# An attention-and-MLP kernel: own-engine waits in front of GpSimd's longer operations

## The chip, the cores and the metric

The kernel runs on one core of a Trainium2 chip. Its time is the device time of one execution, in microseconds. The engines are named as in the profile: PE is TensorE (matmuls; PEld its weight loads), DVE is VectorE, ACT is ScalarE, POOL is GpSimd, and SP is SyncE, which here issues most DMAs.

## What is computed

An "hourglass" attention over 8 batches, 8 heads, 576 positions of 64 channels, whose output is the input of an MLP over 4608 tokens:

```python
q_d = q.reshape(B, H, Sd, 4, D).mean(axis=3)      # k_d, v_d alike: 144 positions
out_up = np.repeat(sm_attn(q_d, k_d, v_d), 4, axis=2)
mask = np.abs(pos[:, None] - pos[None, :]) < 4    # a band of 7 positions
scores = np.where(mask, scale * q @ k.T, -1e9)
attn = softmax(scores)
x = transpose(out_up + attn @ v)                  # 4608 x 512
h = x @ w_in                                      # w_in 512 x 2048
out = (h * sigmoid(h)) @ w_out                    # w_out 2048 x 512
```

## The kernel before

**Tiling.** Two heads of a batch make a pair (32 pairs), two pairs a quad (16 quads). For a pair, q, k and v are loaded by SP into float32 staging buffers (`qs`, `ks`, `vs`; three, three and two of them) and cast to bf16 (`qb`, `kb`, `vb`) by POOL, ScalarE or VectorE. TensorE transposes q and k (from quad 9 on a DMA does), VectorE sums groups of four positions (`qd`, `kd`), TensorE makes the band's scores and the coarse scores in PSUM (tiles `duo`), and ScalarE exponentiates them into `Pt` and `Pd`. VectorE multiplies `Pt` by the band mask in place (`do_mask`, L606 to 611): both its inputs, `Pt` and `mask_bf`, lie in SBUF, 128 x 1152 bf16, 32 times in all. TensorE sums the columns; VectorE takes the reciprocal, which is spread over the partitions by matmuls for the first four quads and, after that, by a store to DRAM (`scr`) and a load back (`Rb`), both issued by SP. TensorE then forms P times V, VectorE multiplies it by `Rb` into `xo`, and POOL adds the two attentions and writes the transposed activations `xT` (`do_add`, L761 to 773).

From quad 4 on the coarse v comes from a second load of v (`vq`) and three additions and a memset on POOL (`castv`, L456 to 465): one addition of 112 x 768 into `vq`, two into `vd`, a memset of part of `vd`.

**The MLP** takes 512 tokens at a time, nine times: 16 blocks `g1` of four matmuls (tile `hps`, at the start also `ops`), a tanh on ScalarE (`th`) and a product on VectorE (`gT`, L794), then 16 blocks `g2` into `ops`, a copy into `osb`, and the store of the output. Its matmuls fill TensorE between those of the attention.

**The order** is not written by hand. Tasks are recorded into one stream per engine by a planner (`choose`, L970 to 985) that estimates each task's start from costs in the code and takes the earliest, with offsets from a table (`TUNE`). The planner treats POOL's operations and the mask product as excluding each other (`self.lock`), in its estimates only.

**Waits** are worked out when an operation is recorded (`Prog.op`, L134 to 200). It collects `deps`, pairs of an earlier operation and a flag; `_dep` (L120 to 132) turns them into semaphore waits. A dependence on the same engine becomes a wait only where the flag is set:

```python
        if d.eng == op.eng and not d.dsem and not forced:
            return
        if know.get(dom, -1) >= val:
            return
```

The flag is set for a tile that the operation reads and an earlier one of its own engine wrote: so the second step of `castv` already waits for the first on POOL's own semaphore. Its third step, which reads the same data as the second, does not wait, and neither does a cast behind a cast. The planner's start estimate `t` (L156 to 159) takes only dependences on other engines and on DMAs into account.

Each operation has a planned `cost` in ns: a POOL cast 680 (L449) or 740 (L454), the steps of `castv` 1900, 1030 and 400 (L460 to 465), an `xT` addition 200 + 1.8 for each column (L772). POOL also issues the loads of the MLP's weights (`load_w`, L823 to 834).

Of the kernel before, what the change touches and what calls it, by code (L numbers as in the profile page):

```python
# [52 lines left out]
class Prog:  # L53
# [38 lines left out]
    def _dma(self, op, eng, t, cost, tau):  # L92

        if t > self.ring_t:
            self._drain(self.rings, self.ring_t, t)
            self.ring_t = t
        full = sum(x[1] / x[2] for x in self.rings[eng]) > 116
        self.rings[eng].append([op, cost, tau, t + (700 if eng == "POOL" else 0)])
        rings = {e: [list(x) for x in q] for e, q in self.rings.items()}
        now, free = self.ring_t, None  # L100
        while any(rings.values()):
            if free is None and (not full or sum(x[1] / x[2] for x in rings[eng]) <= 80 + cost / tau):
                free = now
            now = self._drain(rings, now, now + 400)
        return free or now
# [14 lines left out]
    def _dep(self, op, d, know, forced):  # L120
        if d is op:
            return
        dom, val = (d.dsem, d.dval) if d.dsem else (d.eng, d.pos)
# [4 lines that stand above are left out]
        d.inc = True  # L128
        op.waits = [w for w in op.waits if not (w[0] == dom)] + [(dom, val, d)]
        for k, v in d.K.items():  # L130
            if know.get(k, -1) < v:
                know[k] = v

    def op(self, eng, fn, r=(), w=(), dma=None, cost=0, issue=450, tau=90, lock=False):  # L134
        op = Op(eng, fn)
        op.cost = cost
        op.pos = len(self.streams[eng])
        know = self.know[eng]
        deps = []
        for x in r:  # L140
            if x.psum:
                deps += [(o, False) for e, o in x.last.items() if e != eng]
            else:
                deps += [(o, True) for o in x.writers]
        for x in w:
            if x.psum:
                deps += [(o, False) for e, o in x.last.items() if e != eng]
            else:
                rd = x.readers + ([op] if x in r else [])
                if rd:  # L150
                    x.prev, x.readers, x.writers = rd + x.writers, [], []
                deps += [(o, dma is not None or eng != "PE") for o in x.prev]
                if dma is not None:
                    deps += [(o, True) for o in x.writers if o.dsem != dma]
        deps = [(d, f) for d, f in deps if d is not op]
        t = self.free[eng]  # L156
        for d, f in deps:
            if d.eng != eng or d.dsem:
                t = max(t, d.end + self.LATENCY[d.eng])
        if dma:  # L160
            op.t0 = t
            t += issue if eng == "SP" else 650 if eng == "ACT" else 800
            self.free[eng] = max(t, self._dma(op, eng, t, cost, tau) if eng != "POOL" else t)
            if eng == "POOL":
                self._dma(op, eng, t, cost, tau)
        else:
            if lock or eng == "POOL":
                t = max(t, self.lock)
            op.t0 = t
            self.free[eng] = op.end = t + cost * (1.3 if eng == "PE" and t < 40000 else 1)  # L170
        if lock or (eng == "POOL" and not dma):
            self.lock = op.end
        op.deps = [d for d, f in deps]
        op.tag = self.tag
        deps.sort(key=lambda df: -(df[0].pos if not df[0].dsem else 1 << 30))
        for d, f in deps:
            self._dep(op, d, know, f)
        op.waits = [
            w for w in op.waits
            if not any(v is not w and v[2].K.get(w[0], -1) >= w[1] for v in op.waits)  # L180
        ]
        for x in r:
            if x.psum:
                x.last[eng] = op
            elif x not in w:
                x.readers.append(op)
        for x in w:
            if x.psum:
                x.last[eng] = op
            else:  # L190
                x.writers.append(op)
        op.K = dict(know)
        if dma:
            self.dcount[dma] = self.dcount.get(dma, 0) + 16
            op.dsem, op.dval = dma, self.dcount[dma]
            op.K[dma] = op.dval
        else:
            op.K[eng] = op.pos
        self.streams[eng].append(op)
        return op  # L200
# [848 lines left out]
```

## Time and profile before

| what | us |
|---|---|
| median of 4 runs (lowest, highest) | 374.1 (373.28, 375.96) |
| the profiled execution's own time | 373.87 |
| its span, from the first to the last instruction | 372.1 |
| PE busy, of the span | 340.2 |
| DVE, ACT, POOL busy | 233.3, 217.7, 156.0 |
| POOL's idle time before xT additions, waiting for `xo` of DVE | 59.5 |
| the 32 mask products on DVE, L608 | 29.5 |

The busy shares tell how full each engine is over the whole span. In a list of groups or a timeline, each line gives a start or a count, a duration, the engine, the line of the code, the operation, the tiles as output<-input with their shapes, and in brackets the idle time of that engine just before, with what ended it. Several like instructions in a row are merged and marked x2, x3 and so on. The view of waits gives, for each pair of a waiting group and what it waited for, the total in us, how often, and the longest. The page also has a row of the granted TensorE clock over 40 slices of 9.3 us each:

```profile
PEclk9989699999999999999999999999999999999999
DMA  8999989779999999999996899795144010001012
```

The digits are tenths of full speed and, below, tenths of the 16 DMA engines' time: DMA is near full for the first 200 us.

### The profile page before, as it was taken

The page shows a single profiled execution, that of the slowest core. Times are in us where ns is not written, and L with a number is a line of the kernel's source. Part 1 is how long each engine was busy: PE and PEld are TensorE (multiplying, and loading weights), DVE is VectorE, ACT ScalarE, POOL GpSimd, SP SyncE. Part 2 cuts the span into 40 slices and gives each one's busy share as a digit, 9 for nine tenths or more (in the row PEclk, how much of TensorE's full clock was granted, in tenths as well). Part 3 has the DMA queues.
Part 4 walks back from the last instruction along what each step waited for, and adds up shares of the span by engine and source line. Part 5 has one row for each costly group of instructions (what it writes and reads, how often), then busy time and mean ns, then how long its engine had stood idle before and what let it go on. Part 6 is the DMA issues. An engine that isn't in the chain of part 4 may idle for free.

```text
span 372.1 us, 8309 instructions
## 1 busy us (share of the span) xinstructions
PE 340.2 (91%) x3456; PEld 211.4 (57%) x3498; DVE 233.3 (63%) x375; ACT 217.7 (59%) x362; POOL 156.0 (42%) x203
## 2 busy tenths in 40 slices
PE   0756898999989999999999999999999999999996
PEld 0645566666645665566556565556566555555542
DVE  4688489868668956795598469967765333333310
ACT  4886685576628853886588647766743343443321
POOL 7926672786278429643782285066113000000000
PEclk9989699999999999999999999999999999999999
DMA  8999989779999999999996899795144010001012
GB/s 240 319 361 340 180 224 260 154 202 265 202 242 248 255 256 256 247 234 260 266 235 176 186 196 167 191 168 125 34 116 105 30 56 28 30 28 56 30 56 85
DMA packets 85093, 66.13 MB, mean 178 GB/s; under 512 B 62784, under 2 KB 64832, under 8 KB 85056
## 3 DMA queue, kind: packets, MB, share of 16 engines
q1 hardware_dynamic: 80832, 59.31, 66.5%
q0 software_dynamic: 4224, 6.29, 7.4%
q8 instruction: 27, 0.44, 0.5%
q14 instruction: 10, 0.08, 0.1%
HBM read 53.67 MB, written 9.88 MB: 171 GB/s over the span
## 4 chain that ended last, share of the span: by engine, by line
PE 74%; DMA 9%; DVE 6%; POOL 4%; SPq 3%; issue 2%; ACT 2%; DVEq 0%; POOLq 0%; ACTq 0%
PE ops L538 32%; PE hps L538 31%; PE duo L538 10%; DMA Rb<-scr 4%; DMA scr<-rr 2%; DVE Pt L608 2%; PE duo L548 2%; DMA vq<-in_v_dram 2%; DMA qs<-in_q_dram 1%; SPq L411 1%; POOL xT L771 1%; POOL vq L460 1%; DVE xo L751 1%; POOL vd L462 1%; ACT Pt L585 0%
## 5 line engine op out<-in xcount | busy, mean ns | idle before, releaser
L538 PE MATMUL hps<-xT,w_in_sb 128*128 128x512 f32 x544 | 171.1, 437 | 3.7 <-DVE gT L794 2.4
L794 DVE SCALAR_TENSOR_TENSOR gT<-th,hps 128x512 bf16<-128x512 f32 x136 | 92.5, 682 | 80.9 <-ACT th L792 80.4
L538 PE MATMUL ops<-w_out_bf,gT 128*128 128x512 bf16 x534 | 137.7, 381 | 3.4 <-issue 1.3
L792 ACT ACTIVATE th<-hps 128x512 f32<-128x512 f32 x136 | 81.6, 600 | 97.2 <-PE hps L538 95.1
L538 PEld LDWEIGHTS hps<-xT,w_in_sb 128*128 128x128 f32 x544 | 99.7, 190 | 32.4 <-DVE gT L794 3.3
L538 PEld LDWEIGHTS ops<-w_out_bf,gT 128*128 128x128 bf16 x576 | 46.6, 98 | 68.9 <-issue 28.8
L771 POOL TENSOR_TENSOR xT<-xo 128x576 fp32r<-128x576 f32 (+2 forms) x40 | 39.7, 1004 | 59.6 <-DVE xo L754 59.5
L608 DVE TENSOR_TENSOR Pt<-Pt,mask_bf 128x1152 bf16<-128x1152 bf16 x32 | 29.5, 925 | 6.1 <-ACT Pt L600 5.5
L375 ACT ACTIVATE osb<-ops 128x512 f32<-128x512 f32 x30 | 18.0, 599 | 22.1 <-PE ops L538 22.0
L585 ACT ACTIVATE Pt<-duo 128x912 bf16<-128x912 f32 x29 | 26.9, 929 | 5.7 <-PE duo L538 5.6
L751 DVE TENSOR_TENSOR xo<-duo,Rb 128x456 f32<-128x456 f32 x30 | 18.8, 628 | 14.4 <-DMA Rb<-scr 12.8
L572 DVE TENSOR_REDUCE qd<-qT 128x144 bf16<-128x576 bf16 x29 | 21.4, 746 | 8.4 <-ACT qT L375 5.2
L379 POOL CAST qb<-qs 128x576 bf16<-128x576 f32 x24 | 18.0, 762 | 17.4 <-DMA qr<-qb 15.2
L460 POOL TENSOR_TENSOR vq<-vq 112x768 f32<-112x768 f32 x12 | 22.0, 1836 | 5.3 <-DMA vq<-in_v_dram 5.3
L462 POOL TENSOR_TENSOR vd<-vq 112x384 bf16<-112x384 f32 (+1 forms) x24 | 23.6, 1004 | 1.3
L572 DVE TENSOR_REDUCE kd<-kT 128x144 bf16<-128x576 bf16 x29 | 21.2, 743 | 0.9 <-ACT kT L375 0.7
L379 POOL CAST kb<-ks 128x576 bf16<-128x576 f32 x26 | 16.8, 666 | 11.4 <-PE duo L548 6.2
L379 POOL CAST vb<-vs 128x640 bf16<-128x640 f32 x10 | 7.2, 721 | 24.7 <-PE duo L538 23.6
L375 ACT ACTIVATE vb<-vs 128x640 bf16<-128x640 f32 x20 | 14.5, 736 | 3.3 <-PE duo L538 1.8
L538 PEld LDWEIGHTS duo<-qT,kT 64*128 64x128 bf16 x286 | 8.3, 97 | 12.0 <-issue 4.7
L375 ACT ACTIVATE kT<-kr 128x576 bf16<-128x576 bf16 x12 | 14.9, 1239 | 0.0
L548 PE MATMUL duo<-id_bf,qb 128*128 128x128 bf16 x72 | 5.9, 232 | 9.7 <-ACT qb L375 9.0
(123 smaller groups left out, 332.7 us busy)
## 6 DMA issues: line engine op xcount, KB each, us to landing
vs<-in_v_dram SPq DMA_DIRECT2D x60, 160.0 KB, 5.4
out_dram<-osb SPq DMA_DIRECT2D x36, 256.0 KB, 2.7
Rb<-scr SPq DMA_DIRECT2D x24, 360.0 KB, 5.7
qs<-in_q_dram SPq DMA_DIRECT2D x29, 288.0 KB, 5.2
ks<-in_k_dram SPq DMA_DIRECT2D x29, 288.0 KB, 5.3
vq<-in_v_dram SPq DMA_DIRECT2D x24, 288.0 KB, 5.1
w_in_sb<-in_moe_w_in_dram POOLq DMA_DIRECT2D x4, 1024.0 KB, 12.7
w_out_bf<-in_moe_w_out_dram POOLq DMA_DIRECT2D x4, 512.0 KB, 7.5
```

The costliest lines, as they stand in the source:

```text
L375: fn = lambda e: e.activation(dst, src, AF.Copy, scale=1.0 if scale is None else scale)
L379: fn = lambda e: e.tensor_copy(dst, src)
L460: pool(lambda g: g.tensor_tensor(t, t, z[0:112], ALU.add), r=[R("vq"), R("vqz")], w=[R("vq")], cost=1900)
L462: pool(lambda g, a=a, n=n: g.tensor_tensor(vd[m][0:n, a, :, :, :].rearrange("p i h d -> p h i d"), x[0:n], y[0:n], ALU.add), r=[R("vq"), R ...
L538: return P.op("PE", lambda t: t.matmul(out_, lhsT, rhs, start=start, stop=stop, skip_group_check=True), r, w, cost=cost)
L572: P.op("DVE", lambda e: e.tensor_reduce(dst[j][:, 0:144], src[y][:, :].rearrange("p (g r) -> p g r", r=4), mybir.AxisListType.X, ALU.add), ...
L585: later("ACT", f"e1{p}", [(lambda e: e.activation(Pt[m][:, :, 0:456], D[:, :, 0:456], AF.Exp, scale=0.125), bk, [R(f"P{m}")], 930)], bk)
L608: P.op("DVE", lambda e: e.tensor_tensor(Pt[m][:, :, :], Pt[m][:, :, :], mask_bf[:, :].unsqueeze(1).to_broadcast([128, 2, S_]), ALU.mult), ...
L751: later("DVE", f"pa{p}", [(lambda e: e.tensor_tensor(xo[x][:, 0:456], D[:, 0, 0:456], Rb[u][:, 0:456], ALU.mult), [bk[0], R(f"Rb{u}")], [R ...
L771: P.op("POOL", lambda e, dst=dst, in0=in0, in1=in1: e.tensor_tensor(dst, in0, in1, ALU.add), r=[R(f"xo{x}")], w=xblk(kc, t, e_), cost=200 ...
L792: later("ACT", f"th{n}", [(lambda e: e.activation(th[tb][:, :], hp, AF.Tanh, scale=0.5), [hr], [R(f"th{tb}")], 597)], [hr], pre=[f"st{n - ...
L794: later("DVE", f"st{n}", [(lambda e: e.scalar_tensor_tensor(gT[j % 2][:, f, :], th[tb][:, :], 1.0, hp, ALU.add, ALU.mult), [hr, R(f"th{tb} ...
```

## The change

A POOL operation with a planned cost of 400 or more gets a forced dependence on the operation recorded in front of it on POOL, unless that one is a DMA issue. It then waits, besides all that it waited for, until POOL's semaphore tells that the operation in front has finished.

```diff
@@ -152,6 +152,9 @@
                 deps += [(o, dma is not None or eng != "PE") for o in x.prev]
                 if dma is not None:
                     deps += [(o, True) for o in x.writers if o.dsem != dma]
+        if eng == "POOL" and cost >= 400 and not dma and self.streams["POOL"] and not self.streams["POOL"][-1].dsem:
+
+            deps.append((self.streams["POOL"][-1], True))
         deps = [(d, f) for d, f in deps if d is not op]
         t = self.free[eng]
         for d, f in deps:
```

Since the planner's estimate leaves out dependences on the same engine, the recorded streams keep their order on every engine, and only POOL's operations have other waits than before: of the 191 that are not DMA issues, 129 have one more. Lines behind the change have numbers larger by three.

## The prediction

> **What bounds the kernel now.** I read the busy shares first, then TensorE's (PE's) waits, then the timeline where one of them ends.
>
> ```profile
> PE 340.2 (91%) x3456; PEld 211.4 (57%) x3498; DVE 233.3 (63%) x375; ACT 217.7 (59%) x362; POOL 156.0 (42%) x203
> ```
>
> PE is busy for 340.2 of 372.1 us; POOL, which the change touches, for 42%. From 141 us on PE has no wait above 0.16 us (its busy time is 19.6 to 19.9 in each 20 us). So POOL moves the end only through PE's waits before 141 us, or by making a new one. The view of PE's waits (us in total, times, longest):
>
> ```profile
> PE duo L538 <- DVE Pt L608: 3.5, 2, 2.1
> ...
> PE hps L538 <- DVE gT L794: 2.4, 2, 1.3
> ...
> PE hps L538 <- DVE Pt L608: 1.7, 1, 1.7
> ...
> PE hps L538 <- POOL xT L771: 0.7, 1, 0.7
> ```
>
> 5.2 us are waits for the mask product on VectorE (DVE), L608. The tile's view gives its durations, least, median and longest:
>
> ```profile
> L608 DVE TENSOR_TENSOR Pt<-Pt,mask_bf x32: 742/750/3340, 17.6 to 270.6; 128x1152 bf16<-128x1152 bf16 x32
> ```
>
> Section 5 has 29.5 us for the 32; at 0.75 they would take 24.0. The excess is 5.5 us, and one product holds 2.59 of it. The timeline there:
>
> ```profile
> 53.54 0.73 POOL L379 CAST vb<-vs 128x640 bf16<-128x640 f32 x1
> ...
> 53.97 3.34 DVE L608 TENSOR_TENSOR Pt<-Pt,mask_bf 128x1152 bf16<-128x1152 bf16 x1 [0.79 <-ACT Pt L600]
> 54.20 0.68 POOL L379 CAST qb<-qs 128x576 bf16<-128x576 f32 x1
> ...
> 54.81 0.67 POOL L379 CAST kb<-ks 128x576 bf16<-128x576 f32 x1
> ...
> 55.42 0.66 POOL L379 CAST qb<-qs 128x576 bf16<-128x576 f32 x1
> ...
> 56.03 0.66 POOL L379 CAST kb<-ks 128x576 bf16<-128x576 f32 x1
> ...
> 56.64 1.19 POOL L379 CAST qb<-qs 128x576 bf16<-128x576 f32 x1
> ...
> 57.83 0.74 DVE L608 TENSOR_TENSOR Pt<-Pt,mask_bf 128x1152 bf16<-128x1152 bf16 x1
> ...
> 58.63 0.44 PE L538 MATMUL duo<-Pt,onesZ 128*32 128x72 bf16 x32 [1.45 <-DVE Pt L608]
> ```
>
> The product stands beside a run of six casts. It ends at 57.31, so its 0.75 of work began at 56.56, 0.13 before the fourth cast since its start ends (56.03 + 0.66 = 56.69). The cast after that takes 1.19 instead of 0.66: now POOL waits. PE waits 1.45 us behind the second product, which is queued behind the first.
>
> **The wait's price.** POOL's timeline in two places:
>
> ```profile
> 104.55 1.35 POOL L771 TENSOR_TENSOR xT<-xo 128x384 fp32r<-128x384 f32 x2 [6.03 <-DVE xo L754]
> 105.86 1.83 POOL L460 TENSOR_TENSOR vq<-vq 112x768 f32<-112x768 f32 x1
> 107.84 1.96 POOL L462 TENSOR_TENSOR vd<-vq 112x384 bf16<-112x384 f32 x2
> 109.86 0.41 POOL L465 MEMSET vd<- 64x384 bf16 x1
> 110.24 3.96 POOL L771 TENSOR_TENSOR xT<-xo 128x384 fp32r<-128x384 f32 x6
> ...
> 118.05 1.83 POOL L460 TENSOR_TENSOR vq<-vq 112x768 f32<-112x768 f32 x1 [1.41 <-DMA vq<-in_v_dram]
> 119.96 1.95 POOL L462 TENSOR_TENSOR vd<-vq 112x384 bf16<-112x384 f32 x2
> ```
>
> Without a wait the next operation starts 0.05 before the last one ends: 104.55 + 1.35 = 105.90 against 105.86; two vd of 1.00 each fill 1.96. With a wait for POOL's semaphore alone the gap is 0.08 (118.05 + 1.83 = 119.88, vd at 119.96); where POOL's semaphore comes with another engine's it is 0.15 (107.69 to 107.84). So a new wait costs **0.13 us alone and 0.20 us beside another**, where POOL ran without a gap. Between the two recorded streams 129 of POOL's operations gain it: 43 start after idle time, where the semaphore has long come (nothing), 23 alone and 63 beside others do not. That is 23 x 0.13 + 63 x 0.20 = 15.6 us of POOL's time, against 216 us of idle POOL; only chains that PE waits for count. The order of instructions, and all waits of other engines, stay.
>
> **Does the wait let VectorE in?** The row says that a product was passed over at four handovers with overlap. The Trainium skill (SBUF — State Buffer, "Who interferes with whom") says that whoever starts first has the shared pair for the whole instruction and the other blocks. By that rule the product would wait for the end of one cast (54.27) and end near 54.9; there would be nothing to save, and the same rule makes POOL stand for 0.75 us once VectorE is in, which speaks against the change. By the row 2.4 us of VectorE's time are to be had. I take the row: that a cast already under way overlaps the next is why the pair is never free. With the wait it is free from 0.13 before an end to 0.15 after it, some 0.28 us, and the product is already waiting.
>
> **The path, place by place** (PE's time against before).
> - **41.16: +0.3.** PE waits 0.74 for the xT add of 39.91 to 41.11. Ahead of it kd to xT gets 0.13; xT to qb is hidden, since that cast (1.20 long) stands behind the product of 38.26 anyway, which moves by the same 0.13; qb to xT gets 0.20. Sum 0.33.
> - **58.63: -1.45.** The product starts at 54.3 and ends at 55.1. The second needs its exponentials of 55.55 and, at worst, the end of one cast, and ends by 57.05. PE is free at 57.17 (56.10 + 1.07); it is itself late next, so the gain is PE's whole wait and no more. The run of casts ends 1.3 later, at 59.2 (0.75 for the first product, 4 x 0.20, some 0.3 for the second, less the 0.53 that the last cast stands now); POOL's next work is at 64.72, and the load that waits for the last cast is issued at 59.61. Covered. Now PE stands at -1.15.
> - **77 to 92: +0.45.** Queued behind POOL's waits are casts that free the staging buffers for SP's loads. SP issued the vq load at 82.54 and a ks load at 84.23, each 0.03 after POOL. Summed over the handovers from 76.8 on, these come 0.5 and 0.9 later. Half is taken up at 85.95, where SP waited for ScalarE (85.93). So the scr store (91.14) and its Rb return (landed 103.47), which PE's wait at 105.12 goes back to, come at -1.15 + 0.45 = -0.7.
> - **104 to 112: +0.79.** POOL's run above: 0.13 + 0.20 + 0.13 + 0.20 + 0.13. VectorE's product with Rb at 111.66 waits for its second pair of xT adds (111.59), and PE's score matmuls at 112.3 for the bank. PE is at +0.1 there.
> - **140.25: -0.4.** PE idles 1.01, released by the gT product behind the next Rb landing (138.60):
>
> ```profile
> 140.25 0.97 PE L538 MATMUL hps<-xT,w_in_sb 128*128 128x512 f32 x3 [1.01 <-DVE gT L794]
> ```
>
>  That idle time hides PE's +0.1. SP's queue from 115.14 to the scr store at 126.75 runs without a pause; it started 0.44 after ScalarE's cast of vb (114.70), which hangs on the matmuls at 112.3. So it can come 0.4 earlier and no more: between -0.7 and 0, I take -0.4.
> - **After 141: nothing.** The tightest reader of POOL is VectorE's product at 147.79, 0.76 after its add; four waits ahead of it sum to 0.73. TensorE's readers have 1.7 us or more. If that cover fails, some 0.2 appears once.
> - **Before 38: nothing.** The product of 17.57 (1.23 long) may come 0.2 earlier, but PE then stands 2.1 us at 32.4 with no wait shown. Weight loads issued 0.2 to 0.3 later land 5 us before use.
>
> Sum: 0.3 - 1.45 + 0.45 and what is left of it at 140.25: **-0.4**, so 373.87 - 0.4 = 373.5. The profiled execution stands 0.2 below the median of the runs shown (374.1).
>
> **Rivals.**
> - **All of the gain arrives (0.2): 372.6.** POOL's delays are covered everywhere after 60 us and -1.15 to -1.35 stays. For it: VectorE and ScalarE have slack. Against: SP's waits of 0.03 at 82 to 85.
> - **Slower, through SP's queue (0.2): 375.6.** The scr store was issued 1.5 us after its data was ready (89.60), so SP, with its rings full, sets it, not PE. If PE's gain doesn't move SP's loads ahead, POOL's 0.9 at 84.23 is added to Rb's landing, and PE's wait at 105.12 eats the 1.45. Then 0.9 + 0.79 remain at 112 and no cover at 140.25, as that Rb is late too: +1.7. It decides as soon as the Rb of 103.47 lands after 103.5.
> - **VectorE still isn't let in (0.1): 374.5.** Only costs: 0.3 and some 0.3 at 105. Against: the product of 38.26 got the port between an xT add and a cast with no gap at all.
> - **Faster than the sum (0.08): 371.9.** The early product's 0.5 counts too and nothing is given back: 373.87 - 1.45 - 0.5.
>
> The forecast keeps 0.42. Clock: PE runs at half rate for part of 37 to 47 us (6 tenths in that slice). The skill's "TensorE: Matmul & The Clock Gate", Part 1, gives the gate a free window of 3.4 us; one window more or less is 1.7 us of work, which no row here can exclude; it widens the upper end.
>
> Range 371.9 to 375.4; the forecast's own is 372.9 to 374.1. 0.5% (1.9 us, what a measurement here can tell) puts the bounds at 372.2 and 376.0. Faster: the last rival and a fifth of the first, 0.12. Slower: the upper half of SP's rival and a bad clock window, 0.14. Same: 0.74.
>
> **What would show it.** Right: the product near 54 takes 0.9 to 1.1 us instead of 3.34, PE's 1.45 at 58.6 is gone, POOL's handovers show gaps of 0.08 to 0.15, xT near 41 is 0.3 later. Wrong: a mask product still over 2 us; PE's waits near 105 and 140 longer than 1.3 and 1.0 by more than 0.5; a PE wait above 0.3 after 141.

## The result, and the profile after

| | us |
|---|---|
| before, median of 55 runs (lowest, highest) | 374.48 (370.79, 379.61) |
| after, median of 36 runs (lowest, highest) | 373.25 (370.4, 376.13) |
| ratio after to before, 95% interval | 0.9978 (0.9963 to 0.9993), that is -0.8 us (-0.3 to -1.4) |
| the same, measured again on another occasion | 0.9947 (0.9918 to 0.9977), that is -2.0 us (-0.9 to -3.1) |
| profiled execution: own time, span | 371.63, 369.9 (before 373.87, 372.1) |

Ratios leave disturbed runs out and medians do not, so the two can differ by a little. The change makes the kernel faster by 0.2% to 0.5%: the first interval lies wholly within the 0.5% that counts as no change, the second straddles it. The forecast was 373.5. The two profiled executions differ by 2.24; part of that is chance, as a second profile of before shows further down.

Section 1 of the page of after, busy times:

```profile
PE 339.8 (92%) x3456; PEld 211.5 (57%) x3498; DVE 231.6 (63%) x375; ACT 217.5 (59%) x362; POOL 162.1 (44%) x203
```

POOL is busy 6.1 longer. Busy time counts an overlap of two operations once; all overlaps of neighbours on POOL add up to 4.7 in before and 0.6 in after, and the durations themselves add up to 2.0 more. DVE is busy 1.7 less; the mask products take 27.1 instead of 29.5. PE's waits in after (us in total, times, longest), and the mask product's durations (least, median, longest):

```profile
PE hps L541 <- DVE gT L797: 1.8, 2, 1.2
PE duo L541 <- DVE Pt L611: 1.8, 1, 1.8
...
PE hps L541 <- POOL xT L774: 1.4, 1, 1.4
...
PE duo L541 <- DVE xo L754: 0.7, 1, 0.7
```

```profile
L611 DVE TENSOR_TENSOR Pt<-Pt,mask_bf x32: 745/752/1617, 17.5 to 268.3; 128x1152 bf16<-128x1152 bf16 x32
```

Of the two waits of `duo` for the mask product one is left, the early one. No product is over 1.62. The wait for `xT` is 1.4 instead of 0.7, and a wait for `xo` of 0.7 is new; how much of these two belongs to the change is weighed further down. The timeline of after, where the 3.34 stood before:

```profile
52.83 0.73 POOL L382 CAST vb<-vs 128x640 bf16<-128x640 f32 x1
53.07 1.12 DVE L611 TENSOR_TENSOR Pt<-Pt,mask_bf 128x1152 bf16<-128x1152 bf16 x1 [0.79 <-ACT Pt L603]
53.69 1.02 POOL L382 CAST qb<-qs 128x576 bf16<-128x576 f32 x1
54.71 0.75 DVE L611 TENSOR_TENSOR Pt<-Pt,mask_bf 128x1152 bf16<-128x1152 bf16 x1
54.85 1.14 POOL L382 CAST kb<-ks 128x576 bf16<-128x576 f32 x1
56.12 0.67 POOL L382 CAST qb<-qs 128x576 bf16<-128x576 f32 x1
...
56.22 0.44 PE L541 MATMUL duo<-Pt,onesZ 128*32 128x72 bf16 x32
```

The product ends at 54.19, so its 0.75 began at 53.44, 0.12 before the first cast's end (53.56). The cast of `qb` is issued 0.13 after that end and lasts 1.02 instead of 0.68: now it is the cast that waits for the product. The second product takes 0.75. PE's matmul has no wait ahead of it (no bracket); before it had 1.45. POOL in after, where the price was read from:

```profile
103.58 1.83 POOL L463 TENSOR_TENSOR vq<-vq 112x768 f32<-112x768 f32 x1
105.56 2.08 POOL L465 TENSOR_TENSOR vd<-vq 112x384 bf16<-112x384 f32 x2
107.70 0.41 POOL L468 MEMSET vd<- 64x384 bf16 x1
108.25 4.71 POOL L774 TENSOR_TENSOR xT<-xo 128x384 fp32r<-128x384 f32 x6
```

Two `vd` now take 2.08 together instead of 1.96, and `xT` starts 0.14 after the memset's end where it started 0.03 before it. From the start of `vq` to the start of `xT` it is 4.67 instead of 4.38.

### The profile page after: what moved, and what is told of

It reads as the page before. It is cut to its first block, busy times and chain, and to the rows that moved or that the text cites. A ratio compares the mean times of both kernels' runs of the same rounds, so it can differ in the third digit from the quotient of the medians.

```text
span 369.9 us, 8392 instructions
## 1 busy us (share of the span) xinstructions
PE 339.8 (92%) x3456; PEld 211.5 (57%) x3498; DVE 231.6 (63%) x375; ACT 217.5 (59%) x362; POOL 162.1 (44%) x203
## 4 chain that ended last, share of the span: by engine, by line
PE 79%; DMA 8%; DVE 4%; POOL 4%; ACT 2%; issue 2%; SPq 1%; POOLq 0%; ACTq 0%
PE hps L541 33%; PE ops L541 33%; PE duo L541 10%; DMA Rb<-scr 3%; DMA scr<-rr 3%; PE duo L551 2%; POOL xT L774 2%; DMA qs<-in_q_dram 1%; DVE Pt L611 1%; ACT Pt L588 1%; POOL qb L382 1%; DVE xo L754 1%; POOL vd L465 1%; DVE gT L797 0%; DVE qT L382 0%
## 5 line engine op out<-in xcount | busy, mean ns | idle before, releaser
L611 DVE TENSOR_TENSOR Pt<-Pt,mask_bf 128x1152 bf16<-128x1152 bf16 x32 | 27.1, 853 | 5.7 <-ACT Pt L603 5.5
L382 POOL CAST qb<-qs 128x576 bf16<-128x576 f32 x24 | 18.1, 755 | 17.6 <-DMA qr<-qb 13.7
L465 POOL TENSOR_TENSOR vd<-vq 112x384 bf16<-112x384 f32 (+1 forms) x24 | 24.5, 1020 | 2.2
L382 POOL CAST kb<-ks 128x576 bf16<-128x576 f32 x26 | 18.3, 702 | 12.6 <-PE duo L551 5.3
```

What stands on the lines that cost most here:

```text
L382: fn = lambda e: e.tensor_copy(dst, src)
L465: pool(lambda g, a=a, n=n: g.tensor_tensor(vd[m][0:n, a, :, :, :].rearrange("p i h d -> p h i d"), x[0:n], y[0:n], ALU.add), r=[R("vq"), R ...
L611: P.op("DVE", lambda e: e.tensor_tensor(Pt[m][:, :, :], Pt[m][:, :, :], mask_bf[:, :].unsqueeze(1).to_broadcast([128, 2, S_]), ALU.mult), ...
```

## Experiments

All are made from the changed kernel, by narrowing its condition, or from the kernel before. Each is named by its label, and all ratios are to the kernel before, run on the same chip at the same time.

### Which waits bring it: x1_early, x2_run, x3_late, x4_three

One line is added to the condition. For x2_run:

```diff
-        if eng == "POOL" and cost >= 400 and not dma and self.streams["POOL"] and not self.streams["POOL"][-1].dsem:
+        if eng == "POOL" and cost >= 400 and not dma and self.streams["POOL"] and not self.streams["POOL"][-1].dsem and (
+                self.tag in ("cq9", "ck9", "cq10", "ck10", "cq11")):
```

These five are the casts behind the first one, the value cast, in the run of six near 54. x1_early takes what is recorded ahead of them (15 waits), x3_late what comes behind them (109), and x4_three `("cw2", "cq9", "ck9")`, where `cw2` is the value cast beside the early product near 17.

> The new waits are kept on the 15 operations ahead of the run of six casts and left out on the 114 behind. Own theory (the gain has two places, the run of casts near 54 us and the early product near 17 us; the price is paid at the xT addition near 41 us): the early product is 0.76 instead of 1.23 long, the product near 54 us is again over 2 us long with PE's wait of 1.3 to 1.5 us behind it, and PE's wait for xT near 41 us is longer than 0.74 us by 0.3 to 0.7. Ratio 0.998 to 1.000. Rival (the gain of the whole change lies in these first 50 us): ratio 0.9965 to 0.998 although the product near 54 us stays long.

> The new waits are kept on the five casts behind the first of the run near 54 us alone. Own theory: the product there is 0.9 to 1.2 us long, PE has no wait for it, and as nothing else costs time some 1.2 us arrive at the end: ratio 0.9955 to 0.998. Rival (the 1.45 us are given back at the next wait for an Rb landing, near 105 or 140 us): the product is short too, but PE's wait near 105 us grows from 1.34 to over 2.2 us, ratio 0.999 to 1.001.

> The new waits are kept on the 109 operations behind the run alone. Own theory: the score matmuls near 112 us come 0.6 to 0.8 us later against those before, PE's wait near 140 us shrinks by as much and hides it, SP's loads and the Rb landings stay within 0.3 us: ratio 0.9985 to 1.001. Rival (SP's queue carries POOL's delay of 82 to 85 us into the Rb landings): the Rb of 103.5 us lands 0.4 us later or more and PE's waits near 105 and 140 us do not shrink; ratio 1.001 to 1.004.

> Three waits alone: the cast of vb behind the two copies near 17 us, and the first two casts behind the first of the run near 54 us. Own theory: these two places are all that is to be had. Both long products are 0.75 to 1.1 us, the second product of the run does not wait for more than one cast, the xT addition near 41 us and the matmuls near 112 us cost nothing: faster than the changed kernel, ratio to the kernel before 0.994 to 0.997. Rival (a product is passed over at the handovers that have no wait, here those behind the third cast): the second product of the run is over 1.5 us long and PE waits for it; ratio 0.997 to 0.999.

| kernel | waits | median (runs) | ratio, 95% | product near 54 | PE's wait near 58 |
|---|---|---|---|---|---|
| x1_early | 15 | 375.27 (14) | 1.0001 (0.9971 to 1.003) | 3.53 | 1.63 |
| x2_run | 5 | 373.23 (22) | 0.9964 (0.9937 to 0.9991) | 1.01 | none |
| x3_late | 109 | 374.47 (14) | 0.9998 (0.997 to 1.0026) | 3.42 | 1.53 |
| x4_three | 3 | 373.15 (22) | 0.9978 (0.9954 to 1.0002) | 1.01 | none |

The waits in the run are enough to free the products. The other 124, in two kernels, show neither a gain nor a loss; each of the two intervals reaches some 1.1 us to either side. Two expectations were missed here: PE's wait near 140 did not shrink in x3_late (1.01, as in before), and x4_three was not faster than the changed kernel (0.9978 for both). The timeline of x3_late has the old picture, with the first product over 3 and PE waiting for the second:

```profile
54.11 3.42 DVE L611 TENSOR_TENSOR Pt<-Pt,mask_bf 128x1152 bf16<-128x1152 bf16 x1 [0.78 <-ACT Pt L603]
...
58.86 0.44 PE L541 MATMUL duo<-Pt,onesZ 128*32 128x72 bf16 x32 [1.53 <-DVE Pt L611]
```

### One wait, six waits: x6_one, x7_six

The condition is `self.tag == "cq9"` in x6_one, and in x7_six `cw2` and the five of the run.

> Six waits: the cast of the early value block cw2 and the five casts of the run near 54 us. Theory (the gain lives in the handovers where a product stands waiting, the other waits only cost): both the early product near 17.5 (0.76 instead of 1.23) and the two products near 54 are short, no wait of PE above 0.3 near 58, POOL's chains at 104 to 112 as in the kernel before; time 373.0 to 373.4, ratio about 0.996 to 0.997, at or a little below the changed kernel's 0.9978. Rival (the early waits of the changed kernel carry part of the gain as well): as the five waits alone or worse, 373.4 or more.

> One wait: the first cast of the run, cq9, waits for the value cast ahead of it. Theory (a waiting product is let in where the handover has a gap, and is passed over where casts overlap): the first product takes 1.0 and cq9 stands to 1.02, but the second product, waiting about 1.3 after the first began, meets handovers without a wait: it is passed over and lasts over 1.5, and PE keeps a wait of 0.5 or more near 58; time 374.0 to 374.5. Rival (one early turn is enough, the second product comes through any way): second product 0.75, PE's wait gone, time 373.2 to 373.7 like the five waits.

x7_six: 372.11 (12 runs), 0.9937 (0.9906 to 0.9968), lower than expected, but with 0.996 inside its interval. x6_one: 372.52 (22 runs), 0.9941 (0.9915 to 0.9967). The theory stated for x6_one fell. Its timeline:

```profile
53.02 0.73 POOL L382 CAST vb<-vs 128x640 bf16<-128x640 f32 x1
53.44 0.94 DVE L611 TENSOR_TENSOR Pt<-Pt,mask_bf 128x1152 bf16<-128x1152 bf16 x1 [0.79 <-ACT Pt L603]
53.88 1.02 POOL L382 CAST qb<-qs 128x576 bf16<-128x576 f32 x1
54.85 0.66 POOL L382 CAST kb<-ks 128x576 bf16<-128x576 f32 x1
55.06 1.07 DVE L611 TENSOR_TENSOR Pt<-Pt,mask_bf 128x1152 bf16<-128x1152 bf16 x1
55.46 1.19 POOL L382 CAST qb<-qs 128x576 bf16<-128x576 f32 x1
```

The second product came at 55.06, while the cast of `kb` ran, and there is no wait between that cast and the next: 54.85 + 0.66 = 55.51 against 55.46, the usual overlap of 0.05. Yet it was let in at once (it ended at 55.06 + 1.07 = 56.13, and 56.13 - 0.75 = 55.38 is 0.13 before the cast's end), and the next cast stood (1.19). So an overlap alone does not pass a product over.

That led to a count over all 14 profiles of this study. Taken were the handovers from one POOL operation to the next without a gap, memsets aside, at which a mask product had already been waiting for 0.2 or longer. Outside the run near 54 of the four kernels without a wait there (before, its second profile, x1_early, x3_late), the product was let in at 24 of 24. In those four runs it was passed over at the first four handovers and let in at the fifth, in each of the four.

### Memsets in place of the waits: x5_memset

From the kernel before, with no new wait, and with a memset ahead of three of the casts:

```diff
             for o in self.streams[name]:
+                if name == "POOL" and o.tag in self.junk:
+                    eng.memset(self.junk[o.tag], 0.0)
                 for dom, val, d in o.waits:
...
+        P.junk = {"cq9": osb[1][:, 0:256], "ck9": osb[1][:, 256:512], "cq10": osb[0][:, 256:512]}
```

> The kernel before, without any new wait; instead a memset of a 128 x 256 f32 scratch stretch, which only writes, ahead of each of the casts cq9, ck9 and cq10. Theory G (the product only needs a stretch in which no POOL operation that reads is under way): the first product is let in during the first memset and takes about 1.0 to 1.1, both products together end before 57, PE's wait near 58 falls under 0.4, and the time is 373.3 to 373.9. Rival S (it takes POOL's wait for its own semaphore; operations issued back to back hold the port, whatever they are): the product is over 3 us, PE's wait is 1.4 to 2.2 and the time 374.4 to 375.2.

373.13 (20 runs), 0.9945 (0.9921 to 0.997), as theory G had it (the product needs only a stretch without a POOL operation that reads). Its timeline:

```profile
53.72 0.73 POOL L382 CAST vb<-vs 128x640 bf16<-128x640 f32 x1
54.06 1.16 DVE L611 TENSOR_TENSOR Pt<-Pt,mask_bf 128x1152 bf16<-128x1152 bf16 x1 [0.78 <-ACT Pt L603]
54.37 0.32 POOL L218 MEMSET osb<- 128x256 f32 x1
54.62 1.11 POOL L382 CAST qb<-qs 128x576 bf16<-128x576 f32 x1
```

The work of the product began at 55.22 - 0.75 = 54.47, inside the memset of 54.37 to 54.69, and PE's wait near 58 was gone. The memset overlaps its neighbours by 0.07 to 0.08; most other neighbours on POOL overlap by 0.03 to 0.09. So no wait on a semaphore is needed, and here a memset, which only writes, did not keep the product out. Whether a short operation that reads would have ended the row as well was not tried.

### The kernel before once more: x8_before

> The kernel before once more, for a second profile: how far two executions of the same program lie apart at PE's landmarks. If the executions differ only by chance of the clock and of the loads at the start: the product near 54 again takes 3.3 to 3.5 and PE's wait at 58 is 1.4 to 1.6, while PE's first matmul, the half-clock windows between 21 and 47 us and the xT add near 41 move by some tenths up to 1 us. If the landmarks are the same within 0.2 us everywhere, differences of the profiles of that size are the change's own.

One execution, 371.73, span 370.0. It answers how far two executions of one program lie apart. The product near 54 took 3.42 and PE waited 1.53 behind it, as the first time. The other places where PE waited moved (PE's start times, us; "half rate" is the time between 19 and 50 in which the granted clock was half):

| execution | first matmul | `xT` near 41 | 58.6 | 105 | 112 | 140 | last matmul | half rate |
|---|---|---|---|---|---|---|---|---|
| before | 8.98 | 41.16 | 58.63 | 105.12 | 112.35 | 140.25 | 368.56 | 10.2 |
| x8_before | 7.70 | 39.60 | 57.73 | 103.68 | 110.99 | 138.11 | 366.42 | 17.1 |
| after | 8.92 | 40.73 | 56.22 | 102.53 | 110.45 | 137.98 | 366.30 | 10.2 |
| after, second profile | 8.78 | 41.42 | 56.92 | 102.77 | 111.06 | 139.17 | 367.56 | 13.7 |

The same program ended 2.14 earlier: 1.28 of that was already there at the first matmul (up to 1 was expected), and the waits for `Rb` near 105 and 140 gave another 1.3. On the other side it spent 6.9 more at half rate. The views of the stretches 21 to 25 and 25 to 29 us (start:end, its length, then the busy time of PE, PEld, DVE, ACT and POOL, the granted clock, the DMA share, GB/s), of before and then of x8_before:

```profile
21.00:25.00 4.00, 3.83 (x109) 3.24 (x110) 3.27 (x9) 2.50 (x5) 1.62 (x3) 0.57 1.20 354
25.00:29.00 4.00, 2.34 (x119) 2.16 (x117) 3.14 (x7) 3.00 (x6) 0.00 (x0) 1.00 1.23 348
```

```profile
21.00:25.00 4.00, 2.25 (x40) 1.80 (x42) 3.63 (x8) 3.70 (x8) 0.11 (x1) 0.56 1.21 352
25.00:29.00 4.00, 4.00 (x123) 3.79 (x124) 2.53 (x7) 1.85 (x4) 0.00 (x0) 0.59 1.23 346
```

In before the clock is whole again after 25, in x8_before it is half up to 28.3. So the pair of profiles cannot weigh terms of some tenths; the medians and the local waits have to.

### Why there: y3_dma, z1_fill, with y1_after and y2_one

What the run near 54 has ahead of it is the issue of the fourth block of `w_out` by POOL (52.76 to 53.54 in before); the value cast, with which the run begins, follows it. Behind none of POOL's seven other issues in before did a product wait at a handover, so the trace has this one case. y3_dma is the kernel before with that issue moved behind the last cast of the run, and no new wait. z1_fill is y3_dma with two memsets in the old place of the issue, so that all starts where it did.

```diff
     def emit(self, nc, kctx):
+        s = self.streams["POOL"]
+        s.insert(next(i for i, o in enumerate(s) if o.tag == "cq11"), s.pop(next(i for i, o in enumerate(s) if o.tag == "w5")))
```

```diff
             for o in self.streams[name]:
+                for t in self.junk if name == "POOL" and o.tag == "cw6" else ():
+                    eng.memset(t, 0.0)
...
+        P.junk = osb[1][:, 0:512], osb[0][:, 256:512]
```

y1_after is the changed kernel and y2_one is x6_one, both again, so that they are compared on one chip.

> The changed kernel again, beside the two below on one chip, with a second profile of it. If the five waits near 54 are all that counts, the ratio is 0.995 to 0.998, not better than one wait alone, and xo L754 again stands in the list of PE's waits at 112 (0.7 to 1.2). If the other 124 waits bring something of their own, it is below the kernel with one wait by 0.2% or more.

> The kernel with the single wait at cq9 again. Theory (one gap is enough, the other waits only cost POOL time that is hidden but for some tenths): ratio 0.994 to 0.997, equal to the changed kernel or up to 0.2% better, both products near 54 under 1.3, no wait of PE behind them. Rival (its first measurement was luck, a product is sometimes passed over): a product over 1.5 near 54 and a ratio above 0.998.

> The kernel before without any new wait; only the issue of the fourth block of w_out by POOL, which stands just ahead of the value cast in front of the run near 54, is moved behind the last cast of the run. Theory H (overlapping handovers let a waiting product in everywhere else in these profiles; what is special here is the DMA issue just ahead[...]): the product is let in at its first or second handover, lasts under 1.8, PE's wait near 58 is under 0.5 and the time 373.0 to 373.8, without a single wait. Rival (it is the run of casts as such): the product lasts 2.7 to 3.5, PE waits 1.0 to 1.6, time 374.2 to 374.8. The block lands some 3.9 later, near 63, ahead of the first matmul that reads it.

> As the kernel with the DMA issue moved behind the run, and two memsets of scratch (128 x 512 and 128 x 256 f32, some 0.87 together) in the place where the issue of 0.78 stood, so that the value cast and the run start where they start in the kernel before, and the product arrives during the value cast, as there. Theory H (the DMA issue ahead makes the run pass over a waiting product): the product is let in at the first handover, value cast to cq9, overlapping as it is, lasts 0.9 to 1.3 and PE's wait near 58 is under 0.4. Rival (a product that comes during the value cast is passed over by what follows that cast, DMA or not; with the issue moved it only came one cast later): 3.2 to 3.6 for the product, PE's wait 1.3 to 1.7.

| kernel | new waits | median (runs) | ratio, 95% |
|---|---|---|---|
| y1_after | 129 | 371.88 (9) | 0.9947 (0.9918 to 0.9977) |
| y2_one | 1 | 372.66 (22) | 0.995 (0.9924 to 0.9977) |
| y3_dma | 0 | 372.52 (22) | 0.9954 (0.9932 to 0.9976) |
| z1_fill | 0 | 372.88 (20) | 0.9935 (0.9903 to 0.9966) |

Theory H (the DMA issue ahead makes the run pass a waiting product over) held in both, and y3_dma was faster than the 373.0 to 373.8 expected. The timeline of y3_dma:

```profile
53.67 1.38 POOL L381 CAST vb<-vs 128x640 bf16<-128x640 f32 x2
54.99 0.67 POOL L381 CAST qb<-qs 128x576 bf16<-128x576 f32 x1
55.44 0.83 DVE L610 TENSOR_TENSOR Pt<-Pt,mask_bf 128x1152 bf16<-128x1152 bf16 x1 [0.78 <-ACT Pt L602]
55.60 1.19 POOL L381 CAST kb<-ks 128x576 bf16<-128x576 f32 x1
```

The timeline of z1_fill:

```profile
52.72 0.78 POOL L220 MEMSET osb<- 128x512 f32 x2
53.44 0.72 POOL L384 CAST vb<-vs 128x640 bf16<-128x640 f32 x1
53.84 0.93 DVE L613 TENSOR_TENSOR Pt<-Pt,mask_bf 128x1152 bf16<-128x1152 bf16 x1 [0.78 <-ACT Pt L605]
54.10 1.20 POOL L384 CAST qb<-qs 128x576 bf16<-128x576 f32 x1
```

In both the product is let in at its first handover, which overlaps as ever (55.66 against 55.60; 54.16 against 54.10), and the next cast stands. In y3_dma the product came one cast later than in before, so its place in the run had changed as well; z1_fill has it arrive during the value cast, as in before. z1_fill has memsets ahead, which y3_dma has not. Together, and with one profile of each, they point to the issue in front of the run as what made the run pass the product over.

What it is about the issue stays open. The Trainium skill (SBUF — State Buffer, "SBUF: two separate sides") says that a DMA issued by POOL has its descriptors written by GpSimd, which needs the shared pair. If that writing went on behind the recorded issue and kept VectorE out, x6_one's product would be expected to be kept out too, but it got in at 53.63 (53.44 + 0.94 - 0.75), 0.61 after the issue's end there (53.02). Nor is an issue ahead enough by itself: near 16 us in x6_one three issues stood directly ahead of two copies, and the product that came during the first copy was let in at its end:

```profile
13.75 2.51 POOL L828 DMA_DIRECT2D w_in_sb<-in_moe_w_in_dram  x3
16.24 1.95 POOL L382 COPY gT<-band 128x640 bf16<-128x640 bf16 x2
16.27 1.34 DVE L611 TENSOR_TENSOR Pt<-Pt,mask_bf 128x1152 bf16<-128x1152 bf16 x1
```

(16.27 + 1.34 - 0.75 = 16.86; the first copy ended at 16.99.) That copies and casts differ here was not tried. The casts also wait for a DMA's semaphore each, but so they do in z1_fill, where the product was let in; that alone is not it.

No version is shown to be faster than the changed kernel: one wait and 129 waits give 0.995 and 0.9947 side by side, and none of the intervals is apart from the others.

## Why the prediction was right, and where not

The time and the class were right: 373.5 was forecast, within 0.5% of before; 373.25 and 0.9978 were measured, and the second measurement, 0.9947, lies at the edge of that class. That the time came so close is in part luck: the forecast takes 0.4 off an execution of 373.87, while the median of the 55 runs of before is 374.48. As a difference, 0.4 was forecast and 0.8 (0.3 to 1.4) and 2.0 (0.9 to 3.1) were measured. The forecast's sum gave back 1.05 of the 1.45; the runs suggest that less is given back. The ten measurements in which the product is let in have ratios of 0.9935 to 0.9978, mean 0.9953, which is 1.8 us; but eight of the ten are of kernels with few of the waits or none. So the runs lean to the rival in which all of the gain arrives (372.6), and do not settle it. Step by step:

- **58.63, -1.45: held.** The wait of 1.45 (1.53 in x8_before and in x3_late) is gone in every kernel that lets the product in. The product took 1.12, against a forecast of 0.9 to 1.1. The whole gain is there at PE's next wait, near 77. From the score matmuls ahead of the run to that wait, in before and then in after:

```profile
52.96 0.23 PE L538 MATMUL duo<-qT,kT 64*128 64x120 bf16 x2
77.11 0.68 PE L548 MATMUL duo<-id_bf,qb 128*128 128x128 bf16 x9 [0.64 <-ACT Pt L585]
```

```profile
52.07 0.23 PE L541 MATMUL duo<-qT,kT 64*128 64x120 bf16 x2
74.70 0.68 PE L551 MATMUL duo<-id_bf,qb 128*128 128x128 bf16 x9 [0.64 <-ACT Pt L588]
```

 That is 24.15 and 22.63. In the four profiles that pass the product over it is 24.15 to 24.34, in the ten that let it in 22.63 to 22.65.
- **The reason given for it failed.** The prediction took one row against the rule that whoever starts first has the pair for the whole instruction and the other blocks (the Trainium skill, SBUF — State Buffer, "Who interferes with whom"), and held that a cast under way overlaps the next and so the pair is never free. At 24 of 24 other overlapping handovers the product needed to sit out only the operation under way, which is the rule; the row was the exception, and y3_dma and z1_fill tie it to the DMA issue in front. That a wait lets the product in came true, but not because it takes a gap: the second product of x6_one and the products of x5_memset, y3_dma and z1_fill got in without one, so this step was right in its outcome alone. The prediction's own trace had a witness: the product of 38.26, which got the port with no gap, was put down against a rival only.
- **The price, 0.13 and 0.20: held for POOL; for PE near 41 it can't be seen.** POOL's run near 105 is 0.60 longer from one `xT` start (104.55; 101.96 in after) to the other (110.24; 108.25), by four handovers, where the prediction's prices give 0.66. Near 41 the two `xT` adds start 2.49 apart instead of 2.31, and `kd` to `xT` has a gap of 0.08 instead of an overlap of 0.04: 0.30 in all, against 0.33. What of that reaches PE is lost in chance: its wait there is 1.39 and 1.40 in the two profiles of after, and 0.74 to 1.80 in the eleven profiles of kernels without a wait at this place (0.75 in the execution that the sum was made against).
- **77 to 92, +0.45: not there.** SP's loads did come later against PE, and by more than was forecast: against before, PE stood at -2.41 at 77, the `vq` load came at -1.59 and the `ks` load at -1.19, so 0.8 and 1.2 later. But the store of `scr` was at -1.91 and its `Rb` landed at -2.59 (103.47 before, 100.88 after). The term assumed that a landing keeps the delay of its issue; here the load of `Rb` was issued only 1.12 earlier (95.95, 94.83) and took 6.05 instead of 7.52. In x3_late, too, which has the waits and not the gain, `ks` was issued 1.44 later than in before and `Rb` landed 0.21 earlier. Taken over all profiles, from PE's wait near 77 to this landing it is 25.71 to 26.18 in the three with waits at this place and 25.57 to 26.74 in the eleven without, with means of 25.94 and 25.96. This is the term that was mis-sized, and with it the rival through SP's queue fell: the landing after 103.5 that it named came in none of the three (100.88, 101.12, 103.26).
- **104 to 112, +0.79: +0.70 in after, +0.68 in x3_late.** The chain was the one named; in after VectorE's product waits for `xT` where in before it did not:

```profile
109.76 0.63 DVE L754 TENSOR_TENSOR xo<-duo,Rb 128x456 f32<-128x456 f32 x1 [0.43 <-POOL xT L774]
```

 In the second profile of after the same stretch lost 1.07, and in x7_six and y3_dma, which have no new wait there, 2.29 and 0.49, to a later `Rb`: whichever is last decides.
- **140.25, hidden: held in kind in after.** PE's idle time there shrank from 1.01 to 0.63 and took 0.38 of the 0.70:

```profile
137.98 1.21 PE L541 MATMUL hps<-xT,w_in_sb 128*128 128x512 f32 x4 [0.63 <-DVE gT L797]
```

 Its size is chance: from 112 to 140 the second profile of before gained 0.78 and y3_dma lost 1.67, neither with a wait of this kind.
- **After 141: nothing, as forecast.** From 140 to the last matmul after moved by 0.01, its second profile by 0.08.
- **The clock, 1.7 for one window more: not seen.** x8_before had two such windows more than before, yet from its first matmul to the wait near 41 it took 31.90, and before took 32.18. PE has idle time to lose there: between 19 and 50 it was busy for 24.78 of 31 in x8_before and for 21.98 in before.

What the waits cost in the end lies within the noise: x1_early and x3_late, which between them have 124 of the waits and none of the gain, measured 1.0001 and 0.9998, each within 0.3%.

## What to carry to other kernels

A single long row in a profile is not yet a rule about the port: look for the other places where the same two engines meet in the same trace, and ask what stands ahead of the odd one. Before adding a wait everywhere, try it at the one handover where somebody is waiting; here one wait, three memsets or a DMA issue moved by six operations did what 129 waits did. A delay at the issue of loads need not reach their reader: here 0.8 and 1.2 of it could not be found in the landing that PE waits for. And before a term of some tenths is read from a pair of profiles, look at how far two profiles of one program differ at that place.

## What the runs showed of the hardware that was not expected

- A waiting VectorE product was passed over at four handovers in a row by casts behind a POOL DMA issue, and took 3.3 to 3.5 us in each of four profiles, while at the 24 other overlapping handovers it was let in at once.
- The product (its end less 0.75) begins 0.12 to 0.14 before the recorded end of the POOL operation it waited for, with a wait behind that operation or without; only ahead of the memset of x5_memset did it begin 0.02 after that end.
- PE's half rate between 19 and 50 us comes in pieces of about 3.4, 6.8 and 10.2, and how many differs between executions of one program: 10.2 in all in before, 17.1 in its second profile; 10.2 and 13.7 in after. Three profiles had one more piece later: 112.8 to 116.2 in the second profile of after, 112.1 to 115.5 in x7_six, 143.3 to 146.7 in x1_early. Pieces of that size agree with the window of about 3.4 us that the Trainium skill gives (TensorE: Matmul & The Clock Gate, Part 1).
